# Attention over channels with a gated layer: last pair by subtiles, first v chunk in two halves, batch 0's softmax transposes in the product bank, and new constants of the schedule

## The chip, the cores and the metric

One core of one Trainium2 chip. The metric is the device time of one execution in microseconds; lower is better.

## The reference, cut to what matters

Four batches of q, k and v, each 6336 x 256. Columns of q and k are normalized over the 6336 rows, so the 256 x 256 scores need a whole batch of q and k before any v can be used. The attention output then goes through a gated layer.

```python
qn = q / (norm(q, axis=1) + 1e-6);  kn = k / (norm(k, axis=1) + 1e-6)
a = softmax(kn.transpose(0, 2, 1) @ qn / tau)      # 256 x 256 for each batch
x = (v @ a).reshape(B * S, D)                      # 25344 x 256
H = maximum(x @ w_h, 0);  T = sigmoid(x @ w_t + b_t)
return T * H + (1 - T) * x
```

## The kernel before

For each batch, TensorE forms the Gram matrices of q and k chunk by chunk ("sg"), a chain of small operations turns them into weights that already contain w_h and w_t (`mr`; the norms `inv` are computed on GpSimd), and 25 pairs of row tiles then take three products each ("t", "h", "d"), a tanh and a relu on ScalarE, and two VectorE operations ("pp", then the result "o", or "ot" for the last pair of a batch). There are 100 pairs in all. The Gram matrices of the next batch are interleaved with the pairs of the present one. A scheduler in the kernel's own Python orders all of this by priorities (`PRIO`) and by a model of durations; what it decides is the program.

Loads (to fp16) are issued by GpSimd, in the order of GpSimd's instructions. During a batch's normalization chain no loads are put on GpSimd until the norm is done:

```python
stop = plan.tasks[plan.tasks.index(last) - 3]      # three tasks before the batch's last Gram step
plan.loads_stop.append((stop, nk))                 # no loads on POOL from then until norm nk
```

Stores are issued by SyncE, in order. A chunk's store is held behind a tiny DMA of one row (`held_row`) that waits for a later pair, so that it doesn't take DMA time from the loads. No store is held beyond pair `UNTIL`:

```python
g = ...                       # pair that the store is held for (LAG chunks later)
if g > UNTIL:
    x.key = max(x.key, UNTIL + 1.6)
    continue
plan.add("SP", g + 1.5, ..., lambda n=n: hold(n // NJ, n % NJ), ...)   # held_row <- o
```

In batch 3, v chunks from number `BY_DMA` = 3 on are transposed by DMA ("vT"), also issued by SyncE, `AHEAD` pairs before their first use; earlier chunks are transposed on TensorE ("vtps"):

```python
tr = plan.add("SP", g - AHEAD, ..., loaded("v", b, 2 * i), lambda j=j: transpose_chunk(b, j), ...)
```

## Time and profile before

| | before |
|---|---|
| median of runs | 269.87 us at first; 270.1 us beside the changed kernel |
| span in the profile, granted clock | 268.3 us, 0.997 |
| TensorE busy | 246.4 us (92%) |
| bytes read and written | 78.38 and 25.95 MB, 389 GB/s over the span |
| last result on VectorE ends | 264.57 us |
| last packet of the kernel's own DMAs | 266.8 us |

The profile's lines for these are in the prediction below. In such lines PE is TensorE, PEld its weight loads, DVE VectorE, ACT ScalarE, POOL GpSimd, and SPq the queue of DMAs that SyncE issues; L and a number is a line of the kernel; "x2" means two instructions of the kind, shown as one. The last two rows I worked out from the trace's records of single instructions and packets. From the packets of the loads, stores, holding DMAs and transposing DMAs (queues q0 and q1) I use two more quantities. *Dry time* of a stretch is the time in which fewer than 16 packets were in flight (the core has 16 DMA engines), weighted by the share that was missing: if nothing is in flight for 1 us, that is 1 us dry. The *gap* is the time from the end of the last result to the last packet. Before: 0.70 us dry from 200 to 220 us, 0.43 from 220 to 250, gap 2.2.

### The profile page before, as it was taken

To read this page: it belongs to the slowest core of one execution; us is meant where nothing else is said; L and a number is where in the kernel's file an instruction comes from. 1 tells how busy PE (TensorE), PEld (TensorE's weight loads), DVE (VectorE), ACT (ScalarE), POOL (GpSimd) and SP (SyncE) were. 2 spreads that over 40 slices of the span, in tenths; PEclk is the share of its full clock that TensorE was granted. 3 is DMA by queue.
4 is the path that set the end of the run, shared out by engine and by line. 5 is a ranking of instruction groups with operands and counts; after the bars stand their busy time and mean duration, and the time that the engine had idled before them with its cause. 6 is when DMAs were issued, how large, how long until landed. Compare 5 with 4: busy or idle time off the path is not lost.

```text
span 268.3 us, 6249 instructions
## 1 busy us (share of the span) xinstructions
PE 246.4 (92%) x2430; PEld 216.6 (81%) x2430; DVE 181.6 (68%) x377; ACT 195.1 (73%) x365; POOL 131.7 (49%) x167
## 2 busy tenths in 40 slices
PE   0697977999999999999999999999999999999991
PEld 0596864889989978999999878999998778888880
DVE  1000035777766789557878797586878998998994
ACT  1001016978888789999898887787798999998980
POOL 7233468688778064695689138567655110000000
PEclk9999999999999999999999999999999999999998
DMA  6999999999999999999999999999999999999995
GB/s 107 215 211 208 206 206 202 212 213 214 214 213 212 213 214 255 247 263 269 275 286 258 267 267 254 249 236 281 287 280 239 284 214 304 379 399 165 351 423 232
DMA packets 24622, 67.24 MB, mean 251 GB/s; under 512 B 9104, under 2 KB 11280, under 8 KB 21648
## 3 DMA queue, kind: packets, MB, share of 16 engines
q0 software_dynamic: 13472, 39.20, 75.0%
q1 hardware_dynamic: 11120, 27.64, 29.0%
q8 instruction: 19, 0.31, 0.4%
q14 instruction: 11, 0.09, 0.1%
HBM read 78.38 MB, written 25.95 MB: 389 GB/s over the span
## 4 chain that ended last, share of the span: by engine, by line
PE 76%; DMA 12%; ACT 5%; POOL 2%; issue 2%; DVE 2%; ACTq 0%; DVEq 0%; POOLq 0%
PE h L800 16%; PE t L800 16%; PE d L800 15%; PE sg L452 12%; DMA k<-in_k_dram 10%; PE sg L453 6%; PE vtps L760 5%; DMA v<-in_v_dram 2%; ACT uu L854 2%; PE sg L455 2%; PE t L831 1%; PE vtps L754 1%; PE ah L689 1%; POOL q L327 1%; ACT d L840 1%
## 5 line engine op out<-in xcount | busy, mean ns | idle before, releaser
L800 PEld LDWEIGHTS <-vtsb 128*128 128x128 f16 (+1 forms) x1044 | 98.8, 99 | 17.3 <-issue 3.2
L452 PE MATMUL sg<-q,k 128*128 128x256 f16 x384 | 83.8, 277 | 12.7 <-DMA k<-in_k_dram 12.6
L861 DVE SCALAR_TENSOR_TENSOR pp<-uu,d 128x512 f32<-128x512 f32 (+1 forms) x100 | 68.0, 684 | 28.4 <-PE d L800 16.1
L453 PE MATMUL sg<-k 128*128 128x128 f16 x384 | 76.8, 223 | 0.0
L854 ACT ACTIVATE uu<-t 128x512 f32<-128x512 f32 (+1 forms) x100 | 59.7, 597 | 19.1 <-PE t L800 18.5
L880 DVE SCALAR_TENSOR_TENSOR o<-h,pp 128x512 f32<-128x512 f32 x96 | 65.5, 686 | 1.7
L840 ACT ACTIVATE d<-h 128x512 f32<-128x512 f32 (+1 forms) x100 | 57.9, 584 | 5.7 <-PE h L800 4.9
L800 PE MATMUL t<-mr,vtsb 128*128 128x256 f16 (+1 forms) x348 | 52.2, 272 | 1.5 <-ACT t L533 1.2
L800 PE MATMUL h<-mr,vtsb 128*128 128x256 f16 (+1 forms) x348 | 51.2, 272 | 0.5 <-ACT vtsb L533 0.5
L800 PE MATMUL d<-mr,vtsb 128*128 128x256 f16 (+1 forms) x348 | 51.5, 272 | 0.1
L452 PEld LDWEIGHTS <-k 128*128 128x128 f16 x384 | 38.0, 99 | 16.7 <-DMA k<-in_k_dram 13.9
L476 POOL TENSOR_TENSOR sq<-sq,sq 128x1024 f32<-128x1024 f32 x15 | 35.4, 2361 | 16.7 <-ACT sq L470 16.6
L453 PEld LDWEIGHTS <-k 128*128 128x128 f16 x384 | 38.0, 99 | 1.5
L533 ACT COPY t<-bias_all 128x512 f32<-128x512 f32 (+1 forms) x60 | 35.4, 591 | 1.4
L455 PE MATMUL sg<-q 128*128 128x128 f16 x144 | 32.5, 226 | 0.0
L470 ACT ACTIVATE sq<-q 128x1024 f32<-128x1024 f16 x30 | 31.3, 1053 | 0.0
L760 PE MATMUL vtps<-ident,v 128*128 128x128 f32 x144 | 27.8, 275 | 0.9 <-DMA v<-in_v_dram 0.6
L569 DVE SCALAR_TENSOR_TENSOR junk<-sg,ident 128x128 f32<-128x128 f32 x16 | 4.6, 288 | 33.2 <-PE sg L455 32.7
L535 DVE COPY vtsb<-vtps 128x256 f32<-128x256 f32 (+2 forms) x47 | 19.6, 418 | 7.0 <-PE vtps L760 6.7
L327 POOL DMA_DIRECT2D v<-in_v_dram x24 | 13.7, 571 | 18.9 <-PE vtps L760 11.7
L327 POOL DMA_DIRECT2D q<-in_q_dram x28 | 15.4, 552 | 15.1 <-DMA q<-in_q_dram 7.1
L327 POOL DMA_DIRECT2D k<-in_k_dram x28 | 15.3, 548 | 13.1 <-DMA k<-in_k_dram 9.2
(78 smaller groups left out, 249.5 us busy)
## 6 DMA issues: line engine op xcount, KB each, us to landing
out_dram<-o SPq DMA_DIRECT2D x23, 1024.0 KB, 9.6
v<-in_v_dram POOLq DMA_DIRECT2D x24, 512.0 KB, 16.6
q<-in_q_dram POOLq DMA_DIRECT2D x21, 512.0 KB, 16.2
k<-in_k_dram POOLq DMA_DIRECT2D x21, 512.0 KB, 18.0
q<-in_q_dram POOLq DMA_DIRECT2D x5, 256.0 KB, 9.6
k<-in_k_dram POOLq DMA_DIRECT2D x5, 256.0 KB, 8.9
out_dram<-o SPq DMA_DIRECT2D x2, 512.0 KB, 4.2
out_dram<-ot SPq DMA_DIRECT2D x4, 192.0 KB, 5.1
```

The source lines that it names most:

```text
L327: nc.gpsimd.dma_start(out=t[:, s : s + n, :], in_=main_rows(src)[:, j * CH + s : j * CH + s + n, :])
L452: nc.tensor.matmul(sg[c][:, 0:C], kc, qa, start=first, stop=False)
L453: nc.tensor.matmul(sg[c][:, C : C + P], kc, kc, start=False, stop=False)
L455: nc.tensor.matmul(sg[c][:, C + P : C + 2 * P], qa[:, cs], qa[:, cs], start=False, stop=last)
L476: add(out=sq, in0=sq, in1=other)
L533: nc.scalar.copy(out=out, in_=in_)
L760: nc.tensor.transpose(ps[:, u, 0:nr], v.bitcast(f32), ident0[0:nr, 0:nr])
L800: nc.tensor.matmul(out[0:nr, u, :], vt[u][kt][:, 0:nr], mr[kt][:, col * C : (col + 1) * C], **flags(u, kt))
L840: nc.scalar.activation(out=d[0:nr, :, :], in_=ps_t["h", b, i][0:nr, :, :], func=Act.Relu, scale=0.5)
L854: nc.scalar.activation(out=uu[0:nr, :, :], in_=ps_t.pop(("t", b, i))[0:nr, :, :], func=Act.Tanh, scale=-0.5)
L861: nc.vector.scalar_tensor_tensor(out=pp[0:nr, :, :], in0=el.pop(("uu", b, i))[0:nr, :, :], scalar=1.0, in1=ps_t.pop(("d", b, i))[0:nr, :, ...
L880: nc.vector.scalar_tensor_tensor(out=ot, in0=ps_t.pop(("h", b, i))[0:nr, :, :], scalar=0.0, in1=el.pop(("pp", b, i))[0:nr, :, :], op0=AluO ...
```

## The change

Its intent is to start batch 0's products earlier, to shorten the last pair, and to let a searched set of constants use both. The few words that describe it speak of v's first chunk in one load; the diff turns one load into two halves, and the diff decides.

```diff
-UNTIL = 73
-AHEAD = 16
+UNTIL = 79
+AHEAD = 14
-V_AHEAD = 2
+V_AHEAD = 4.5
 PRIO = {                          # all 12 rows new, cut
-HEAD = 5.5
+HEAD = 8.5
-ENDS = [18, 48.5, 62.25]
+ENDS = [15, 45.25, 55.75]
...
-    for s in range(0, CH, CH // 2):
-        plan_load("q", 1, 0, s, CH // 2)
-        plan_load("k", 1, 0, s, CH // 2)
+    plan_load("q", 1, 0, 0, CH // 2)
+    plan_load("k", 1, 0, 0, CH // 2)
     w_ld = [ ... ]
+    plan_load("v", 0, 0, 0, CH // 2)
+    plan_load("q", 1, 0, CH // 2, CH // 2)
+    plan_load("k", 1, 0, CH // 2, CH // 2)
+    plan_load("v", 0, 0, CH // 2, CH // 2)
-    plan_load("v", 0, 0)
...
+        e_tag = "vt" if b else "h"
-                st["eps"] = new("vt", [P, 2, 2, P], f32, f"eps{b}")
+                st["eps"] = new(e_tag, [P, 2, 2, P], f32, f"eps{b}")
...
+            halves = [slice(0, 1), slice(1, 2)] if g == NP * B - 1 else [slice(0, 2)]
+            if len(halves) > 1:
+                x0 = plan.add("PE", pr("x", g), 0.22, 0.42, [r], lambda i=i: main_x(b, i, [0]), follows=[t])
...                                # x, product and result once for each of halves
```

More of the change, by code (lines that the diff above doesn't have):

```diff
@@ L27 @@
 APART = 5
-V_AHEAD = 2
+V_AHEAD = 4.5
 PRIO = {
-    "tr": (24.974, 16.445, 34.195, 63.304),
-    "ev": (74.59, 73.008, 67.512, 50.704),
-    "h": (-53.39, -86.015, -64.208, -14.641),
-    "bias": (-28.394, 23.065, -1.772, 4.453),
-    "t": (4.111, -1.918, 67.766, 74.312),
-    "relu": (46.555, -20.175, -1.498, 14.915),
-    "x": (0.958, -19.433, 43.343, -6.4),
-    "gate": (-54.132, 37.28, -94.231, -112.222),
-    "prod": (-40.861, -10.819, -26.763, -55.482),
-    "res": (53.604, 18.42, 116.457, -9.113),
-    "s1": (117.419, 42.459, 84.45),
-    "sq": (-15.195, 72.384, 19.395),
+    "tr": (19.428, 22.476, 8.035, 45.128),
+    "ev": (69.463, 40.349, 60.85, 41.167),
+    "h": (-23.962, -62.908, -34.855, -3.659),
+    "bias": (-48.672, 12.93, -28.532, -14.121),
+    "t": (-8.79, 4.089, 54.782, 110.199),
+    "relu": (-13.546, -59.067, -42.065, -16.352),
+    "x": (5.646, -1.233, 62.394, -12.508),
+    "gate": (-65.246, 50.122, -110.921, -86.913),
+    "prod": (-59.013, 4.061, -25.159, -55.436),
+    "res": (2.958, -50.391, 111.288, -83.467),
+    "s1": (107.218, 50.191, 87.67),
+    "sq": (-21.111, 64.498, 54.142),
 }
 POW = 0.75
-HEAD = 5.5
+HEAD = 8.5
 TAIL = 66
 EV = BIAS = ("ACT", "DVE")
-ENDS = [18, 48.5, 62.25]
+ENDS = [15, 45.25, 55.75]
 class Ring:
@@ L710, in plan_chain @@
         for c in range(2):
-            tr = pe(lambda c=c: trans(c), 0.22, [ex[c]] + et, take=["vt"] if c == 0 else [])
+            tr = pe(lambda c=c: trans(c), 0.22, [ex[c]] + et, take=[e_tag] if c == 0 else [])
             tr0 = tr if c == 0 else tr0
@@ L715, in plan_chain @@
                     lambda e, c=c: evac_et(c, e), (0.29, 0.35), (0.42, 0.47), [tr] + et,
-                    drop=[(tr0, "vt")] if c else [],
+                    drop=[(tr0, e_tag)] if c else [],
                 )
@@ L789, in evac_vt, with products @@
             ]
-    def products(out, b, i, col, flags):
+    def products(out, b, i, col, flags, us=(0, 1)):
         mr, vt, nr = mr_t[b], vt_sb[(b, i)], rows(2 * i)
-        for u in range(2):
+        for u in us:
             for kt in range(2):
@@ L842, in relu, with main_x @@
         )
-    def main_x(b, i):
+    def main_x(b, i, us):
         products(
             ps_t["d", b, i], b, i, 0,
-            lambda u, kt: dict(start=False, stop=u == 1 and kt == 1, skip_group_check=True),
+            lambda u, kt: dict(start=False, stop=u == 1 and kt == 1, skip_group_check=True), us,
         )
-        del vt_sb[(b, i)]
     def gate(b, i):
@@ L856, in gate, with product @@
         )
-    def product(b, i):
+    def product(b, i, us):
         nr = rows(2 * i)
-        el["pp", b, i] = pp = new("pp", [P, 2, C], f32, f"pp{b}_{i}")
+        if us.start == 0:
+            el["pp", b, i] = new("pp", [P, 2, C], f32, f"pp{b}_{i}")
         nc.vector.scalar_tensor_tensor(
-            out=pp[0:nr, :, :],
-            in0=el.pop(("uu", b, i))[0:nr, :, :],
+            out=el["pp", b, i][0:nr, us, :],
+            in0=el["uu", b, i][0:nr, us, :],
             scalar=1.0,
-            in1=ps_t.pop(("d", b, i))[0:nr, :, :],
+            in1=ps_t["d", b, i][0:nr, us, :],
             op0=AluOp.add,
@@ L868, in product, with result @@
         )
-    def result(b, i):
+    def result(b, i, us):
         nr, s = rows(2 * i), 2 * i
         if s >= S:
-            og[(b, NJ)] = new("ot", [P, 2, C], f32, f"ot{b}")
-            ot = og[(b, NJ)][0:nr, :, :]
+            if us.start == 0:
+                og[(b, NJ)] = new("ot", [P, 2, C], f32, f"ot{b}")
+            ot = og[(b, NJ)][0:nr, us, :]
         else:
@@ L881, in result @@
             out=ot,
-            in0=ps_t.pop(("h", b, i))[0:nr, :, :],
+            in0=ps_t["h", b, i][0:nr, us, :],
             scalar=0.0,
-            in1=el.pop(("pp", b, i))[0:nr, :, :],
+            in1=el["pp", b, i][0:nr, us, :],
             op0=AluOp.max,
@@ L1011, in plan_stage2 @@
             r = plan.add("ACT", pr("relu", g), 0.5, 0.63, [h] + set_d, lambda i=i: relu(b, i), take=["d"])
+            halves = [slice(0, 1), slice(1, 2)] if g == NP * B - 1 else [slice(0, 2)]
+            if len(halves) > 1:
+                x0 = plan.add("PE", pr("x", g), 0.22, 0.42, [r], lambda i=i: main_x(b, i, [0]), follows=[t])
             x = plan.add(
-                "PE", pr("x", g), 0.43, 0.63, [r], lambda i=i: main_x(b, i), follows=[t],
+                "PE", pr("x", g), 0.43 / len(halves), 0.63 - (0.22 if halves[1:] else 0), [r],
+                lambda i=i, us=[1] if halves[1:] else [0, 1]: main_x(b, i, us),
+                follows=[x0 if halves[1:] else t],
                 drop=([(tr, vt_tag)] if last_of else [])
@@ L1020, in plan_stage2 @@
             )
-            m = plan.add(
-                "DVE", pr("prod", g), 0.6, 0.72, [x, u], lambda i=i: product(b, i), take=["pp"],
-                drop=[(r, "d"), (u, "uu")],
-            )
             s = 2 * i
@@ L1027, in plan_stage2 @@
             tag = "ot" if s >= S else "o"
-            y = plan.add(
-                "DVE", pr("res", g), 0.6, 0.72, [m] + ([own_o] if 0 < o and s < S else []),
-                lambda i=i: result(b, i),
-                take=[tag] if s >= S or o == 0 else [], drop=[(h, h_bank), (m, "pp")],
-            )
+            y, f = None, 1 / len(halves)
+            for us in halves:
+                whole = us.stop == 2
+                m = plan.add(
+                    "DVE", pr("prod", g), 0.6 * f, 0.6 * f + 0.12, [x if whole else x0, u],
+                    lambda i=i, us=us: product(b, i, us), take=["pp"] if us.start == 0 else [],
+                    drop=[(r, "d"), (u, "uu")] if whole else [],
+                )
+                m0 = m if us.start == 0 else m0
+                y = plan.add(
+                    "DVE", pr("res", g), 0.6 * f, 0.6 * f + 0.12, [m] + ([own_o] if 0 < o and s < S else []),
+                    lambda i=i, us=us: result(b, i, us),
+                    take=[tag] if (s >= S or o == 0) and us.start == 0 else [],
+                    drop=[(h, h_bank), (m0, "pp")] if whole else [],
+                )
+                y0 = y if us.start == 0 else y0
             if s >= S:
                 plan.add(
-                    "SP", g + 2, 0.1, 0, [y], lambda: store(b, NJ, 0, 2), drop=[(y, "ot")],
+                    "SP", g + 2, 0.1, 0, [y], lambda: store(b, NJ, 0, 2), drop=[(y0, "ot")],
                     size=TR * 2 * C * 4,
```

## The prediction

> **What bounds the kernel now**
>
> I read the page's shares first, then its forty slices, the queue totals, the windows by stage, the waits, and last the timelines of the two places that the change names: the first products of batch 0 and the last pair.
>
> The page. TensorE is busy 92% and always has the full clock; the DMA row is 9 from the second slice to the last but one.
>
> ```profile
> span 268.3 us, 6249 instructions
> PE 246.4 (92%) x2430; PEld 216.6 (81%) x2430; DVE 181.6 (68%) x377; ACT 195.1 (73%) x365; POOL 131.7 (49%) x167
> ...
> DMA  6999999999999999999999999999999999999995
> GB/s 107 215 211 208 206 206 202 212 213 214 214 213 212 213 214 255 247 263 269 275 286 258 267 267 254 249 236 281 287 280 239 284 214 304 379 399 165 351 423 232
> ...
> q0 software_dynamic: 13472, 39.20, 75.0%
> q1 hardware_dynamic: 11120, 27.64, 29.0%
> ...
> HBM read 78.38 MB, written 25.95 MB: 389 GB/s over the span
> ```
>
> The reader is to see two resources full at once. A slice with loads alone moves 206 to 215 GB/s as they arrive (fp16, so twice that is read from HBM); the best slice near the end, where stores prevail, moves 423. At 213 the 39.2 MB of loads take 184 us, at 423 the 25.95 MB of stores 61 us: 245 us of 268.3, and the transposing DMAs come on top (the slice with 165 GB/s has one). Queue shares 75 + 29 are over 100%.
>
> By stage (length, busy time of the engines, granted clock, DMA share, GB/s):
>
> ```profile
> 0.00:2.50 2.50, 0.00 (x0) 0.00 (x0) 0.00 (x0) 1.28 (x1) 1.47 (x7) 1.00 0.00 0
> 37.00:46.00 9.00, 5.89 (x48) 4.10 (x49) 5.85 (x25) 4.44 (x10) 7.33 (x11) 1.00 1.14 201
> 46.00:100.00 54.00, 53.37 (x526) 47.21 (x524) 39.17 (x80) 46.09 (x84) 36.60 (x44) 1.00 1.07 213
> 220.00:260.00 40.00, 39.99 (x376) 34.61 (x375) 36.92 (x60) 36.54 (x71) 1.04 (x2) 1.00 1.05 327
> 260.00:265.00 5.00, 2.34 (x19) 1.80 (x17) 4.37 (x7) 1.60 (x4) 0.00 (x0) 1.00 0.89 364
> 265.00:268.30 3.30, 0.00 (x0) 0.00 (x0) 0.00 (x0) 0.00 (x0) 0.00 (x0) 0.78 0.35 117
> ```
>
> DMA is idle for 2.5 us at the start, 0.55 us (0.11 of 5) from 260 to 265, and 2.1 us (0.65 of 3.3) after, where the last store's end and receipt lie. Everywhere else it is full. So whatever TensorE gains, only some 1 to 2 us at the end can be given back, unless DMA itself does less.
>
> The two places of the change (start, duration, engine, instruction, idle time before it):
>
> ```profile
> 44.77 0.41 PE L760 MATMUL vtps<-ident,v 128*128 128x128 f32 x2 [0.63 <-DMA v<-in_v_dram]
> 45.65 0.61 PE L800 MATMUL h<-mr,vtsb 128*128 128x256 f16 x4 [0.46 <-ACT vtsb L533]
> ...
> 43.42 1.51 DVE L702 TENSOR_SCALAR mr<-ah,ri 128x512 f16<-128x512 f32 x2
> ...
> 262.57 0.69 DVE L880 SCALAR_TENSOR_TENSOR o<-h,pp 128x512 f32<-128x512 f32 x1
> 263.18 0.67 DVE L861 SCALAR_TENSOR_TENSOR pp<-uu,d 96x512 f32<-96x512 f32 x1
> 263.89 0.69 DVE L880 SCALAR_TENSOR_TENSOR ot<-h,pp 96x512 f32<-96x512 f32 x1
> ```
>
> Above, batch 0's weights are ready at 43.42 + 1.51 = 44.93, but the first product waits until 45.65 for a v chunk, its transpose and its copy. Below, the last pair's two VectorE operations follow the pair before without a gap.
>
> **What the Trainium skill says**
>
> "DMA: Bandwidth & Descriptors", section "Issuing engines are not separate DMA queues": DMAs of all issuing engines run on the same 16 DMA engines and interleave. The windows agree: share about 1.06 whether loads run alone (213 GB/s) or mixed. Its section "Measured" has 425 GB/s for 16 MB in one go; the 423 of the store slice agrees. "Perfetto Trace Analysis", section "Identifying the Most-Contended Engine": judge DMA by HBM utilization and don't trust matmul busy; so I take TensorE's stalls from start-to-start distances. "VectorE: DVE Perf Modes", section on the TRN2 errata: each operation pays a fixed cost. The trace agrees: 288 ns for 128 columns, 684 for 512, hence some 0.16 us fixed and 1.03 ns per column.
>
> **The change part by part**
>
> The few words say that v's first chunk comes in one load; the diff does the reverse (one load becomes two halves), and I go by the diff. Far more of it is new constants of the scheduler, which move nearly every instruction.
>
> *First v chunk in halves, ahead of batch 1's second half chunk.* Before, it was issued at 38.88, behind GpSimd's norm, and landed at 44.64 behind 2 q/k halves (1.25 us each by their landings) and two weights. Now half of it stands before them, so it lands about when the k half did, near 40.8. The total of bytes up to the next q/k chunk is the same, so k's second chunk still lands near 49.5.
>
> *Transposes of the softmax into the product bank.* The v bank is free, so TensorE's order becomes: v transpose 0, softmax transpose, v transpose 1, softmax transpose, two folds, 8 Gram matmuls, first products. The chain is: softmax transposes at about 41.4 and 41.8, copies, second fold near 43.0, second weight copy ended near 44.2. First product at 44.3 instead of 45.65: 1.35 us. But 8 Gram matmuls less (0.66 us) lie before it and one transpose more (0.22): 0.9 us of work-equal gain. Then the single t bank (matmuls 0.44 us, activation 0.60, bias copy 0.59, with latencies about 1.95 us a turn) and k's chunk at 49.5 hold it: at 49.6 TensorE has done one group of four matmuls more (0.44) and is 0.2 us earlier. I take 0.65 us.
>
> *Schedule at the later chains.* TensorE's waits of over 0.15 us after 50 us add up to about 5 us; they stand where there is no Gram work between two t groups and the t bank turns: at batch 2's chain 0.49 and 0.87 us beyond dense issue, of which the timeline shows
>
> ```profile
> 153.61 0.60 PE L800 MATMUL t<-mr,vtsb 128*128 128x256 f16 x4 [0.28 <-ACT t L533]
> 155.58 0.60 PE L800 MATMUL t<-mr,vtsb 128*128 128x256 f16 x4 [0.65 <-ACT t L533]
> ```
>
> In the new order 12 Gram matmuls stand before the second of these; two shorter bank turns remain (0.35 and 0.15): gain 0.8 us. Batch 1's chain: about 0.2. Batch 3's: its order trades one for another, 0. Together 1.0 us, uncertain to 1 us either way.
>
> *Last pair by subtiles.* Of its four x matmuls only the last signals in the built program, so the first half product waits for both halves: nothing starts earlier. VectorE now runs 4 operations of 0.42 (estimate: 0.16 + 256 x 1.03 ns) at 0.35 apart, 1.47 us, for 2 that took 1.40: cost 0.07 us.
>
> *More stores held back (limit 73 to 79, two more of the tiny holding DMAs), transposing DMAs asked for 2 pairs later.* No bytes change; what changes is when the DMA engines might run dry.
>
> Sum on TensorE and VectorE: 0.65 + 1.0 - 0.07 = about 1.6 us earlier at the last product. At the end the stores meet it: DMA has 0.55 us idle before 265 and perhaps 0.5 of the 2.1 after it, plus a few tenths around the transposes. So about 1.0 us of the 1.6 is paid out: 269.87 - 1.0 = 268.9 us.
>
> **The rivals**
>
> *DMA takes all of it.* If the last stores are as late as before because the DMA work in front of them is the same and never ran dry, the end moves 0 to 0.3 us: 269.6 to 269.9. For it: the 9s of the DMA row. Against: the idle 0.55 us before 265, which is a producer's delay.
>
> *Holding more stores leaves a hole.* Between about 205 and 233 us the loads run out while five or six chunks (1 MB, some 2.45 us each) wait for pair 79, 6 pairs of 1.42 us after pair 73. If DMA is dry for 2 us there, the backlog ends that much later: 270.5 to 271.5, and a transposed v chunk that stands behind those stores may stop TensorE. For it: loads already run short near 210 (slices 239 and 214 GB/s). Against: I count 23 us of loads, stores and transposes left for these 26.
>
> *The new schedule removes nearly all stalls.* Then TensorE ends 4 to 5 us earlier, and DMA's floor of about 267 us holds it: 267.3. For it: constants that look searched. Against: the floor.
>
> **Range and chances**
>
> The first rival and the main line fill 268.2 to 269.9; the second pulls the top to 270.6, the third the bottom to 267.3. I predict 268.9 us, 8 in 10 from 267.3 to 270.6. Over 2% faster would be below 264.5, under the floor that I see: 0.02. Over 2% slower would be above 275.3 and need a DMA hole of 5 us: 0.02. Within 2%: 0.96.
>
> **What would show it right or wrong**
>
> Right: first product of batch 0 near 44.3, no wait for v before it; the wait of t for ACT's bias copy shorter near 153; the two half products back to back after the last x matmul; DMA share 1.0 or more in all stages from 2.5 us until about 264; a span 0.7 to 1.3 us shorter. Wrong: a DMA share clearly under 1 between 200 and 235 (second rival), TensorE waiting for a transposed v chunk near the end, or a span under 266 us, which would mean that DMA moves its bytes in less time than I hold possible. If the first product is earlier and the span is not, DMA or the later chains took the gain.

## The result, and the profile after

| | before | after |
|---|---|---|
| median (lowest to highest), 6 runs each | 270.1 us (269.4 to 270.6) | 273.75 us (272.07 to 275.61) |
| ratio, 95% interval | | 1.0135 (1.009 to 1.0179) |
| span of the profiled run, clock | 268.3 us, 0.997 | 272.3 us, 0.994 |
| dry 200 to 220, 220 to 250 us | 0.70, 0.43 | 2.74, 0.65 |
| last result, last packet, gap | 264.57, 266.8, 2.2 | 265.80, 271.0, 5.2 |

A ratio here is the mean time of one kernel's runs over that of the other's runs of the same rounds, so it is not quite the ratio of the medians. The change is inside the class "within 2%", but clearly slower, by 1.35%, and 273.75 lies above the range of 267.3 to 270.6 us.

Page of the kernel after:

```profile
span 272.3 us, 6251 instructions
PE 246.5 (91%) x2430; PEld 216.1 (79%) x2430; DVE 183.3 (67%) x380; ACT 195.1 (72%) x364; POOL 132.3 (49%) x168
...
DMA  6999999999999999999999999999996999999996
GB/s 111 214 210 208 206 198 195 212 214 217 213 212 210 213 221 281 227 270 241 274 281 260 263 277 269 234 265 246 287 289 217 146 325 198 288 383 400 243 412 249
```

TensorE's work is the same. The DMA row has a 6 in its 31st slice, where the row of before has a 9. That slice is 204 to 211 us. The windows around it, before (length, busy time of the engines, granted clock, DMA share, GB/s):

```profile
205.00:210.00 5.00, 4.72 (x44) 3.98 (x44) 4.72 (x21) 4.57 (x11) 1.96 (x3) 1.00 1.01 283
210.00:215.00 5.00, 4.97 (x39) 3.71 (x37) 4.71 (x13) 4.54 (x13) 0.00 (x0) 1.00 1.03 273
215.00:220.00 5.00, 4.88 (x42) 3.96 (x41) 4.65 (x9) 4.94 (x11) 0.53 (x1) 1.00 1.12 221
```

and after:

```profile
205.00:210.00 5.00, 4.88 (x42) 3.83 (x41) 4.59 (x17) 4.56 (x11) 1.30 (x2) 1.00 0.76 261
210.00:215.00 5.00, 5.00 (x43) 4.19 (x42) 4.79 (x18) 4.80 (x15) 1.19 (x3) 1.00 0.74 129
215.00:220.00 5.00, 4.99 (x45) 4.03 (x44) 4.76 (x9) 5.00 (x11) 0.53 (x1) 1.00 1.03 235
```

The compute engines are as busy as before. Only the DMA share has fallen, to 0.76 and 0.74: the loads ran dry. What GpSimd did then says why. Its timeline before (start, duration, engine, instruction, idle time before it):

```profile
198.38 0.57 POOL L327 DMA_DIRECT2D v<-in_v_dram  x1 [2.71 <-PE vtps L760]
...
207.25 0.71 POOL L580 TENSOR_TENSOR inv<-x,half 128x2 f32<-128x2 f32 x1 [2.94 <-DVE x L606]
...
209.04 0.60 POOL L327 DMA_DIRECT2D v<-in_v_dram  x1
```

and after:

```profile
203.65 0.73 POOL L489 TENSOR_TENSOR sums<-sums,sq 128x256 f32<-128x256 f32 x1
208.26 0.71 POOL L583 TENSOR_TENSOR inv<-x,half 128x2 f32<-128x2 f32 x1 [3.88 <-DVE x L609]
...
210.05 1.14 POOL L327 DMA_DIRECT2D v<-in_v_dram  x2
```

Before, chunk 2 of batch 3's v is asked for at 198.38, as soon as TensorE has freed its buffer, ahead of the last squares. After, it stands behind the norm and is asked for at 210.05, together with chunk 3. The data and the buffer allowed more: in e5 below the same load goes out at 200.56. The Gram work of batch 3 ends two pairs earlier in the new order (its last matmul starts at 202.68 us, before at 205.68), so in the scheduler's plan the stop of loads begins before the buffer comes free. The load is asked for 11.7 us later than before (experiment e5 will show that 9.5 of them are the displacement alone), and the DMA engines run out of work.

SyncE's queue before:

```profile
215.27 3.13 SPq L768 DMA_TRANSPOSE vT<-v  x1
219.55 0.54 SPq L919 DMA_DIRECT2D held_row<-o  x1
...
264.60 0.33 SPq L892 DMA_DIRECT2D out_dram<-ot  x1
```

and after:

```profile
219.93 0.50 SPq L923 DMA_DIRECT2D held_row<-o  x1
...
221.30 6.67 SPq L771 DMA_TRANSPOSE vT<-v  x1
...
237.50 0.53 SPq L923 DMA_DIRECT2D held_row<-o  x1
238.07 4.63 SPq L898 DMA_DIRECT2D out_dram<-o  x5
242.81 11.75 SPq L771 DMA_TRANSPOSE vT<-v  x1
...
265.82 0.33 SPq L896 DMA_DIRECT2D out_dram<-ot  x1
```

The first transposing DMA is 6.0 us later and now behind a held store; the third one waits behind five stores that are let go together at 238. Its chunk lands late, and TensorE waits for it. (The late load has a part in this too: in e2, e3 and e6 below, with `AHEAD` 16, the first transposing DMA starts at 218.8 to 219.0, about 3.6 us late.) TensorE's timeline after:

```profile
256.67 0.61 PE L803 MATMUL h<-mr,vT 128*128 128x256 f16 x4 [1.35 <-DMA vT<-v]
```

That moves the last result from 264.57 to 265.80. But the end moves by 4 us, because the last store, asked for at 265.82, has its last packet only at 271.0. The window of the end, after:

```profile
265.00:272.30 7.30, 0.00 (x0) 0.00 (x0) 0.80 (x3) 0.00 (x0) 0.00 (x0) 0.76 0.66 257
```

From 265 us on nothing but the last results is computed, and the DMA engines still move 257 GB/s over 7.3 us, 1.9 MB (257 x 7.3), where before it was 117 over 3.3 us, 0.4 MB. The two places that the change is named for look as follows after. The first products of batch 0 (TensorE) and the weights before them (VectorE):

```profile
44.98 1.29 PE L803 MATMUL h<-mr,vtsb 128*128 128x256 f16 x8
```

```profile
43.87 1.41 DVE L705 TENSOR_SCALAR mr<-ah,ri 128x512 f16<-128x512 f32 x2 [0.26 <-PE ah L692]
```

The wait for v is gone. And the last pair on VectorE:

```profile
264.39 0.74 DVE L864 SCALAR_TENSOR_TENSOR pp<-uu,d 96x256 f32<-96x256 f32 x2
265.05 0.74 DVE L884 SCALAR_TENSOR_TENSOR ot<-h,pp 96x256 f32<-96x256 f32 x2
```

From the start of the first half product to the end of the last half result 1.41 us passed; the two whole operations of before took 1.39 us from 263.18.

### The profile page after: what moved, and what is told of

It is laid out like the page before. It is cut to its first block, busy times and chain, and to the rows that moved or that the text cites. A ratio compares the mean times of both kernels' runs of the same rounds, so it can differ in the third digit from the quotient of the medians. Undisturbed runs are those within 1.5% of the kernel's fastest.

```text
span 272.3 us, 6251 instructions
## 1 busy us (share of the span) xinstructions
PE 246.5 (91%) x2430; PEld 216.1 (79%) x2430; DVE 183.3 (67%) x380; ACT 195.1 (72%) x364; POOL 132.3 (49%) x168
## 4 chain that ended last, share of the span: by engine, by line
PE 65%; DMA 19%; DVE 4%; ACT 3%; POOL 3%; issue 2%; SPq 2%; DVEq 0%; ACTq 0%; POOLq 0%
DMA k<-in_k_dram 13%; PE t L803 13%; PE h L803 12%; PE sg L454 12%; PE d L803 12%; PE sg L455 6%; DMA vT<-v 5%; PE vtps L763 5%; DVE pp L864 2%; ACT uu L856 2%; SPq L898 2%; PE sg L457 2%; DVE o L884 1%; POOL k L327 1%; POOL q L327 1%
## 5 line engine op out<-in xcount | busy, mean ns | idle before, releaser
L454 PE MATMUL sg<-q,k 128*128 128x256 f16 x384 | 81.6, 275 | 13.2 <-DMA k<-in_k_dram 13.1
L864 DVE SCALAR_TENSOR_TENSOR pp<-uu,d 128x512 f32<-128x512 f32 (+2 forms) x101 | 68.0, 678 | 27.1 <-PE d L803 15.1
L455 PE MATMUL sg<-k 128*128 128x128 f16 x384 | 75.7, 222 | 0.0
L537 DVE COPY vtsb<-vtps 128x256 f32<-128x256 f32 (+2 forms) x49 | 20.4, 416 | 9.4 <-PE vtps L763 9.0
```

The costliest lines, as they stand in the source:

```text
L454: nc.tensor.matmul(sg[c][:, 0:C], kc, qa, start=first, stop=False)
L455: nc.tensor.matmul(sg[c][:, C : C + P], kc, kc, start=False, stop=False)
L864: nc.vector.scalar_tensor_tensor(out=el["pp", b, i][0:nr, us, :], in0=el["uu", b, i][0:nr, us, :], scalar=1.0, in1=ps_t["d", b, i][0:nr, u ...
```

## The experiments

Two theories. *D*: the DMA engines bound the end, and every microsecond in which they ran dry is paid there. *T*: TensorE's wait for the transposed chunk sets the end, by way of the last result. The expectations use more letters: H and N are D with a cause named for the dry time (H the stores held to pair 79, N the place of v's load), H2 is H as a rival to N, and C is any other part of the change. Beside them stood the question of which part of the change does it: a code part, or which constant.

All results first. "Dry" is from 200 to 250 us; times in us from the profiled run; fourteen kernels ran.

| run | ratio to before (95%) | dry | last result | last packet | gap |
|---|---|---|---|---|---|
| before | 1 | 1.13 | 264.57 | 266.8 | 2.2 |
| after | 1.0135 (1.009 to 1.0179) | 3.39 | 265.80 | 271.0 | 5.2 |
| e1_until73 | 1.0106 (1.0068 to 1.0144) | 2.83 | 268.82 | 270.6 | 1.8 |
| e2_ahead16 | 1.0111 (1.0068 to 1.0153) | 3.52 | 264.21 | 270.6 | 6.4 |
| e3_both | 1.0076 (1.0032 to 1.012) | 3.27 | 267.68 | 270.5 | 2.8 |
| e4_struct | 1.0618 (1.058 to 1.0656) | 5.84 | 282.95 | 284.7 | 1.8 |
| e5_v2first | 1.0069 (1.0027 to 1.0111) | 3.02 | 264.11 | 269.3 | 5.2 |
| e6_before_v2late | 1.0177 (1.0135 to 1.0219) | 2.85 | 267.26 | 271.8 | 4.6 |
| e7_fixed_all | 0.9964 (0.9907 to 1.002) | 0.81 | 264.22 | 266.9 | 2.7 |
| e8_before_nostop | 0.9989 (0.9948 to 1.0031) | 1.23 | 265.17 | 267.0 | 1.8 |
| e9_bydma4 | 1.0064 (1.0005 to 1.0123) | 3.70 | 266.04 | 268.6 | 2.5 |
| e10_nosplit | 0.9974 (0.9925 to 1.0023) | 0.80 | 263.91 | 265.7 | 1.8 |
| e11_fixed_bydma4 | 0.9997 (0.9947 to 1.0047) | 2.24 | 264.49 | 266.3 | 1.8 |
| e12_before_bydma4 | 1.0151 (1.0087 to 1.0216) | 4.63 | 270.39 | 272.9 | 2.5 |
| e13_nostop_until73 | 1.0064 (1.0008 to 1.012) | 3.29 | 266.68 | 269.7 | 3.0 |
| e14_nostop_ahead16 | 1.0057 (0.9979 to 1.0134) | 1.64 | 263.71 | 268.0 | 4.3 |

### The two constants alone: e1, e2, e3

On the kernel after, one or both of the SyncE constants put back:

```diff
-UNTIL = 79      # e1 and e3
+UNTIL = 73
-AHEAD = 14      # e2 and e3
+AHEAD = 16
```

> The changed kernel with one constant back (stores held until pair 73 instead of 79). Theory H (holding more stores leaves the DMA engines dry near 210 us, 2.7 us in the changed kernel's trace, and that backlog is what ends the run): 269.0 to 270.5 us, DMA idle between 200 and 215 under 1 us, the last store lands within 3.5 us of its issue. Rival T (only the order of the last transposing DMAs behind five released stores counts): also faster, since the stores are released before those transposes, so 269 to 270.5 and no wait of TensorE for vT near 255; T and H part in the next run. Rival C (the other constants or the three code parts cost the time): 272 or more.

> The changed kernel with the transposing DMAs asked for 16 pairs ahead again; the holding limit stays at 79. The last whole transposed chunk now stands ahead of the five released stores in the store queue. Theory H: the dry spell near 210 us and the backlog at the end stay, 271.5 to 273.5 us, though TensorE's wait for vT is gone. Rival T: 269 to 270.5 us.

> The changed kernel with both constants back (73 and 16); priorities, pacing of the loads, v ahead 4.5 and the three code parts stay new. H and T alike: 268.5 to 270 us. Rival C: 272 or more, since what costs is still in.

None of the three gets back to the kernel before, so both theories were wrong on e3 (268.5 to 270 us were expected). H was wrong on e1: the dry time from 200 to 215 us, expected under 1 us, was 2.7. e2 decides between D and T. TensorE waits for no transposed chunk there, and the last store is asked for earlier than before, yet the end stays late. SyncE's queue and the window of the end, e2:

```profile
264.24 0.33 SPq L896 DMA_DIRECT2D out_dram<-ot  x1
```

```profile
265.00:272.30 7.30, 0.00 (x0) 0.00 (x0) 0.00 (x0) 0.00 (x0) 0.00 (x0) 0.50 0.58 235
```

After 264.24 nothing is computed, and 1.7 MB (235 GB/s over 7.3 us) are still to be moved. T falls as what sets the end of this kernel. In e1 it is the other way about: stores let go at pair 73 stand before the transposing DMA, the last result comes as late as 268.82, and the gap is the least possible. So either can come last, and putting one constant back trades one for the other. The dry time from 200 to 220 us, 2.5 to 2.7 us, is the same in all three: it is not owed to these constants.

### The code parts alone: e4

The code of after with all of before's constants (`UNTIL`, `AHEAD`, `V_AHEAD`, `PRIO`, `HEAD`, `ENDS`).

> The three code parts alone, all constants as before. If they are worth what I predicted (first product about 0.65 us of work earlier, last pair 0.07 us dearer, DMA idle at the end paying out part of it): 269.2 to 270.0 us. Rival C in its form 'the code parts cost': 272 or more.

6% slower, which says nothing on the code parts: e7 below runs the same code with the new priorities and pacing at 0.9964, so they fit this code and the old ones don't. Pairs late in the kernel took 2.07 us (two in 4.13) where they take 1.42. Its VectorE timeline:

```profile
258.44 0.69 DVE L864 SCALAR_TENSOR_TENSOR pp<-uu,d 128x512 f32<-128x512 f32 x1 [1.40 <-PE d L803]
...
262.57 0.69 DVE L864 SCALAR_TENSOR_TENSOR pp<-uu,d 128x512 f32<-128x512 f32 x1 [1.40 <-PE d L803]
```

The opposite mix, before's code with after's constants, could not be built: the scheduler found no task that it could start. The same holds for the v halves alone. The softmax transposes in the product bank alone do build, but were not run.

### Is it the order of the v load? e5, e6, e8

e5 is the kernel after, e8 the kernel before, with batch 3's loads never stopped:

```diff
-        plan.loads_stop.append((stop, nk))
+        if b < B - 1:
+            plan.loads_stop.append((stop, nk))
```

e6 does to the kernel before what the change did: the stop begins one task earlier in batch 3, so that the load of v chunk 2 falls behind the norm.

```diff
-        plan.loads_stop.append((stop, nk))
+        plan.loads_stop.append((plan.tasks[plan.tasks.index(last) - 4] if b == B - 1 else stop, nk))
```

> The changed kernel, but batch 3's chain no longer stops the loads, so the load of v chunk 2 of batch 3 stands ahead of GpSimd's norm in its queue (in the changed kernel it stands behind it and is issued at 210.05 us, 11.7 us after the same load of the kernel before). Theory N (this order left the DMA engines dry near 208 to 212 us, and in a program whose DMA is full to the end every such microsecond is paid at the last store): idle time there under 0.8 us in place of 2.6, and 1.5 to 3 us off the changed kernel's time, a ratio to the kernel before of 1.000 to 1.006. Rival H2 (what ends the run is the stores held until pair 79): no change, ratio about 1.011 to 1.013.

> The reverse on the kernel before: its loads are stopped one subtile earlier in batch 3, which puts the same load (v chunk 2 of batch 3) behind the norm and nothing else of the loads. Theory N: the engines run dry near 208 us for 2 to 3 us, and the time rises by 1.5 to 3 us, ratio 1.006 to 1.012. Rival H2 or C: ratio 0.998 to 1.003.

> The kernel before with the loads not stopped at batch 3's chain, so v chunk 3 of batch 3 too stands ahead of the norm. By theory N it takes away the 0.56 us of idle time that the kernel before has near 210 us: ratio 0.996 to 1.000. If the norm now waits behind a load that waits for its buffer, TensorE stalls at batch 3's chain and the ratio is over 1.003.

e6 is the strongest of all: one task's difference in the stop costs the kernel before 1.77%, more than the 0.6 to 1.2% expected. In its trace every engine has the same instructions in the same order as before, but for this one load. GpSimd's timeline of e6 shows the load in after's place:

```profile
208.62 0.69 POOL L580 TENSOR_TENSOR inv<-x,half 128x2 f32<-128x2 f32 x1 [0.44 <-DVE junk L569]
209.26 1.14 POOL L327 DMA_DIRECT2D v<-in_v_dram  x2
```

its windows the same hole:

```profile
205.00:210.00 5.00, 4.72 (x45) 4.03 (x44) 4.59 (x19) 4.54 (x11) 2.10 (x4) 1.00 0.70 245
210.00:215.00 5.00, 4.97 (x40) 3.77 (x38) 4.77 (x14) 4.54 (x13) 0.40 (x1) 1.00 0.94 156
```

and TensorE the same late wait, for 2.3 us (the first transposing DMA starts 3.6 us later than before, at 218.84, though `AHEAD` is still 16):

```profile
251.60 0.61 PE L800 MATMUL t<-mr,vT 128*128 128x256 f16 x4 [2.30 <-DMA vT<-v]
```

In e5 the load is back in its place, 9.5 us ahead of after's 210.05 and ahead of the norm; chunk 3's load, at 204.14, is ahead of it too. TensorE, VectorE and SyncE keep after's order. GpSimd's timeline of e5:

```profile
200.56 0.57 POOL L327 DMA_DIRECT2D v<-in_v_dram  x1
...
207.46 0.71 POOL L583 TENSOR_TENSOR inv<-x,half 128x2 f32<-128x2 f32 x1 [2.76 <-DVE x L609]
```

That gives back about half of the loss (1.0135 to 1.0069, just above the expected 1.000 to 1.006; the two intervals overlap a little; e8 shows that the same edit is worth nothing where the order was right already). From 206 to 213 us the dry time falls from 2.55 to 0.33 us, as expected. Not all comes back, because in e5 the engines run dry a little later instead, 1.77 us from 213 to 220. Windows of e5:

```profile
210.00:215.00 5.00, 4.99 (x41) 3.96 (x40) 4.87 (x14) 4.81 (x13) 0.00 (x0) 1.00 0.93 277
215.00:220.00 5.00, 5.00 (x46) 4.08 (x44) 4.71 (x10) 4.96 (x11) 0.58 (x1) 1.00 0.70 161
```

The loads now end in time, but the first transposing DMA, which before followed them at 215.27, is asked for only at 220.29 with `AHEAD` 14.

### Load order and constants together: e7, e13, e14

e7 is e5 with both constants of before; e13 is e5 with `UNTIL` 73 alone, e14 e5 with `AHEAD` 16 alone.

> The changed kernel with the load ahead of the norm, the stores held to pair 73 and the transposing DMAs 16 pairs ahead. Theory N with the two earlier suspects as small terms: ratio 0.996 to 1.002. If the ratio stays above 1.007, the loss is in something that none of the three touches.

> The changed kernel with batch 3's loads never stopped and the stores held to pair 73 as before; the transposing DMAs still asked for 14 pairs ahead. If the hole near 212 us (2 us dry) that stayed when the loads alone were mended is owed to holding the stores to pair 79: the DMA share from 210 to 220 us rises above 1.0 from 0.82, and if that is all, ratio 0.996 to 0.999. If the transposes then stand behind the earlier stores and TensorE waits for a transposed chunk (as it did with 73 in the unmended kernel), the hole goes but ratio 1.000 to 1.006. I expect the second.

> The changed kernel with batch 3's loads never stopped and the transposing DMAs asked for 16 pairs ahead as before; the stores still held to pair 79. If holding the stores makes the hole: the share from 210 to 220 us stays near 0.8 and the end stays late though no chunk is waited for: ratio 1.002 to 1.007. If the late asking for transposes was what remained: ratio 0.996 to 0.999.

e7 gives everything back: 0.9964. The priorities, the pacing of loads and the code parts are still new in it, so rival C falls: they cost nothing that shows, except by where they put the load. Windows of e7, to be read against those of e5:

```profile
210.00:215.00 5.00, 4.99 (x41) 3.94 (x40) 4.86 (x16) 4.81 (x13) 0.00 (x0) 1.00 0.94 294
215.00:220.00 5.00, 5.00 (x45) 4.08 (x44) 4.71 (x10) 5.00 (x11) 0.58 (x1) 1.00 1.17 208
```

with SyncE's queue:

```profile
214.64 3.48 SPq L772 DMA_TRANSPOSE vT<-v  x1
```

By the profiles each constant has its own hole. With `AHEAD` 14 the first transposing DMA comes 6 us later and the engines run dry at 216 to 218 us. Windows of e13, then of e14, from 210 to 220 us:

```profile
210.00:220.00 10.00, 9.99 (x86) 8.22 (x85) 9.54 (x25) 9.81 (x25) 0.67 (x2) 1.00 0.74 209
```

```profile
210.00:220.00 10.00, 9.99 (x85) 8.02 (x83) 9.58 (x24) 9.79 (x23) 0.58 (x1) 1.00 1.02 249
```

So my expectation that `UNTIL` 73 would close the hole near 212 us was wrong: `AHEAD` closes it. (TensorE did wait 0.8 us for a transposed chunk in e13, as expected.) With `UNTIL` 79 the stores are still held near 238 us, when the transposing DMAs in front of them are done and nothing else is left. Windows of e14, then of e7:

```profile
236.00:240.00 4.00, 4.00 (x40) 3.51 (x39) 3.48 (x7) 3.81 (x8) 0.00 (x0) 1.00 0.83 197
```

```profile
236.00:240.00 4.00, 4.00 (x40) 3.51 (x39) 3.48 (x7) 3.81 (x9) 0.00 (x0) 1.00 1.04 428
```

e14 and e7 differ in `UNTIL` alone. e14's last result is 0.5 us earlier, and its last packet 1.1 us later: that much of the stores was held for too long. The timed ratios of e14 and e7 (1.0057 and 0.9964) have intervals that overlap, so this last part rests on the profile. It also is not a plain sum: with the loads mended, either constant alone gained nothing that the timing can tell from e5's 1.0069.

### Taking work off the DMA engines: e9, e11, e12

One transposing DMA fewer in batch 3 (two chunks and the tail instead of three), its chunk transposed on TensorE. e9 is on after, e11 on e7, e12 on before.

```diff
-BY_DMA = 3
+BY_DMA = 4
```

> The changed kernel with one transposing DMA fewer in batch 3 (two of its v chunks are left to them where three were), the chunk transposed on TensorE instead. That takes about 4.4 us of the 16 DMA engines' time and puts about 0.9 us on TensorE. My theory (the DMA engines bound the end: they ran dry near 208 us and again around the released stores, and each dry microsecond is paid at the end): 2 to 3 us come back, ratio to the kernel before 1.001 to 1.006. Rival (TensorE's wait for a transposed chunk and its own work set the end): the wait of 1.35 us goes but 0.9 us of work is added, so the time hardly moves, ratio 1.010 to 1.014.

> The changed kernel with batch 3's loads never stopped, the two constants of before, and one transposing DMA fewer in batch 3. Theory that the DMA engines set the end of that kernel too (last result at 264.3, last store's packets at 266.9): the last packets come up to 2 us earlier until TensorE's work, longer by 0.9 us, sets the end; ratio 0.991 to 0.997. Rival that TensorE sets it already: 0.9 us slower than without, ratio 0.998 to 1.001.

> The kernel before with one transposing DMA fewer in batch 3 and nothing else. Its last result comes at 265.3 and its last store is asked for at 264.6, so the producers and the DMA engines end nearly together: 4.4 us less DMA work against 0.9 us more TensorE work. If DMA alone bounds it: up to 2 us faster, ratio 0.993 to 0.997. If TensorE's chain sets the last store: 0 to 0.9 us slower, ratio 1.000 to 1.004. I expect the middle, 0.997 to 1.002.

e9's profile tells D from T for the kernel after itself (its timed interval alone, 1.0005 to 1.0123, does not exclude T's 1.010). Its last store is asked for 0.24 us later than after's, and its last packet comes 2.4 us earlier; the ratio falls from 1.0135 to 1.0064. SyncE's queue and the window of the end, e9:

```profile
266.06 0.33 SPq L896 DMA_DIRECT2D out_dram<-ot  x1
```

```profile
265.00:272.30 7.30, 0.00 (x0) 0.00 (x0) 1.04 (x4) 0.00 (x0) 0.00 (x0) 0.60 0.33 123
```

In e11, where nothing stood in the last store's way (gap 1.8), it bought nothing, 0.9997: the last result sets that end, and TensorE has 16 matmul instructions more to do (2446 against 2430). So e11 went with the rival, and its 2.24 us of dry time cost nothing that shows: with less DMA work the older stores were through by the last result all the same, so not every dry microsecond is paid. e12 missed what I expected. (The 265.3 in its expectation is a slip; the last result of before ends at 264.57.) Its profiled run had a late v load in the head that cost it 2.9 us, which the timed runs need not share; from pair 80 to 99 it lost 3 us more than before did, as e4 did, in waits among TensorE, ScalarE and VectorE. My guess, not tested, is that priorities fitted to three transposing DMAs don't suit two. It says nothing on DMA.

### The split of the last pair: e10

e7 without it:

```diff
-            halves = [slice(0, 1), slice(1, 2)] if g == NP * B - 1 else [slice(0, 2)]
+            halves = [slice(0, 2)]
```

> The changed kernel with batch 3's loads never stopped and the two constants of before (which ran at 0.996), without the last pair's split. Theory: the split buys nothing, since the last x matmul alone signals, and costs about 0.07 us on VectorE; so ratio 0.995 to 0.998, the same as with the split within 0.002. Rival (the half products and results do start earlier and shorten the tail): this run is 0.3 us or more slower than its twin, ratio 0.998 to 1.000.

0.9974 without, 0.9964 with it: the same. The split is worth nothing that these runs can show.

No version was found that beats both kernels with certainty. e7 and e10 are the best, 0.3 to 0.4% under before, with intervals that contain 1.

## Why the prediction was right or wrong

*What bounds the kernel.* Right: TensorE and DMA are both full, and what TensorE gains does not reach the end while stores are behind. It was DMA that decided. (The skill's 425 GB/s is a figure for loads, the 423 beside it one of stores; they agree as numbers only.)

*Batch 0's head.* Right in its mechanism. In e7, which has the same head, the first product starts at 44.14 (predicted 44.3), and no product waits for v. In the profile of after itself the norm came 0.8 us later than before (38.32 against 37.52), so it shows 44.98. (In e7 the v transpose ahead of the softmax's still waits 0.71 us for the v half; that lies where the chain isn't ready anyway.) But the 0.65 us that I booked for it did not come: up to 50 us TensorE's stalls are 9.7 us before and 9.8 us in e14. (A stall is here what the distance from one matmul's start to the next has over the median distance for its shape in before. Another yardstick moves the sums, but their differences by less than 0.3 us.) TensorE only did products in place of Gram work.

*Later chains.* The named wait near 153 us is gone, and stalls from 150 to 160 us fell from 1.5 to 0.5 us (e14), as predicted. From 130 to 150 they rose from 0.1 to 0.9. From 50 us to the end the sum fell by 0.5 us, not 1.0. Together TensorE's stalls fell by some 0.5 us (16.4 to 15.9) instead of 1.65; the last results of e7, e10 and e14 come 0.35, 0.66 and 0.86 us before before's.

*Last pair.* Right in that nothing started earlier, at a cost of 0.02 us for 0.07 predicted. The reason given, that the first half product waits for both halves, is not shown: VectorE was busy with the pair before until the half product began at 264.39, after the last x matmul (263.44 + 0.60).

*What the end makes of it: here it failed.* The step is "So about 1.0 us of the 1.6 is paid out", and under it, in the second rival, "Against: I count 23 us of loads, stores and transposes left for these 26". I had written the right test, whether the DMA engines run dry between 205 and 233 us, and then answered it by adding up bytes. 23 us of work for 26 us even says that a hole is possible; and a sum says nothing on when each transfer can start. Two transfers started later. One v load moved from 198.4 to 210.05, behind GpSimd's norm: I compared the order on TensorE and VectorE between the two kernels, but not on the engine that issues the loads. And the first transposing DMA moved from 215.27 to 221.30. The change of `AHEAD`, which I had listed as "asked for 2 pairs later" and given no cost, is enough for most of that (220.29 in e5, with the load in time), and the late load alone for a part (218.84 in e6). The hole so came at 206 to 213 us (2.55 us dry) from the late loads; behind it lay one at 213 to 220 from the late transpose, which shows once the loads are mended (e5, 1.77 us). The held stores, which I had named as the cause, added a smaller one near 238. I gave this rival 270.5 to 271.5 us, and named both of its signs, a share under 1 and a wait for a transposed chunk. The signs came, with a loss 2 us larger; the cause that I gave for them carries only the smaller hole.

*Sizes.* From before to after the last packet moved by 4.2 us. Dry time from 200 to 250 us explains 2.3 us of it (3.39 - 1.13). In e6 it is 1.7 of 5.1 us (2.85 - 1.13, and 271.8 - 266.8); there TensorE's wait for the chunk has moved the last result by 2.7 us. Over the whole run the load packets' own times, summed and divided by 16, grew by 1.8 us (201.2 to 203.0) with the same bytes; they vary from 200.2 to 203.3 between these runs. Why they take longer in the runs with holes, and with it a part of the loss, stays open.

## What to carry to other kernels

Where DMA bounds a kernel, compare two versions first by the order in which each engine issues its transfers, not by their bytes: a load that falls behind a computation on its issuing engine can leave the DMA engines short of work, and what is lost in the middle comes out as a backlog of stores at the end. To find out whether the end is set by work or by backlog, look at the time from the last result to the last packet, and take some DMA work away. And constants that were searched for one code are part of that code; change one alone and you measure the misfit.

## What the Trainium skill lacked or had wrong

- "DMA: Bandwidth & Descriptors", section "Issuing engines are not separate DMA queues", says that issuing on several engines saves only the sequencer's time to start a DMA, usually small. That section does not say that a DMA also waits for all that stands before it on its issuing engine; what other pages say of queues and waits is not brought together with it, and none gives a size. Here that was worth 9.5 us for one load (210.05 in after, 200.56 in e5), and in e6 the same displacement alone cost 1.77%.
- The same page, section "Latency and other measured facts", gives 261 GB/s for transposing DMAs (350 to 400 where contiguous). Here 1.67 MB of them, in packets of 256 bytes, took 12.5 us of all 16 engines' packet time before, 12.4 after: about 134 GB/s (1.67 MB / 12.5 us). They ran in part beside stores, and the same bytes took 11.4 us in e2 and 14.2 in e7, so this is rough; but planning with the page's figure would give about half of their cost.
- "Perfetto Trace Analysis", section "Identifying the Most-Contended Engine", judges DMA by HBM utilization. Over the span that fell from 389 to 383 GB/s, 1.5%, which is the loss itself and not its cause. The share by windows of 5 us, 0.76 and 0.74 against 1.01 and 1.03, showed where it was.
